# One-core attention and channel mix: shorter weight conversion, one 64-column transpose for the last keys, a split first gate, new load order

## The chip, the cores and the metric

The kernel runs on one core of a Trainium2 chip. The metric is the device time in microseconds of one execution; shown is the median of several. The core's engines are TensorE (PE; its weight loads are the rows PEld), VectorE (DVE), ScalarE (ACT), GpSimd (POOL) and SyncE (SP), which here issues nearly all DMAs. Each engine runs its own instructions in order and waits for others by semaphores. Sums of matmuls land in PSUM.

## The reference, cut to what matters

```python
B, H, S, D = 8, 8, 576, 64;  pool = 8
k_p = k.reshape(B, H, 72, 8, D).mean(axis=3)          # 72 pooled keys per head
v_p = v.reshape(B, H, 72, 8, D).mean(axis=3)
attn = softmax(q @ k_p.T / sqrt(D))                   # 576 x 72 per head
x = (attn @ v_p), heads side by side                  # 8 x 576 x 512
x_prev = x shifted by one position along the sequence (zeros first)
xk = mu_k * x + (1 - mu_k) * x_prev
xr = mu_r * x + (1 - mu_r) * x_prev
h = relu(xk @ w_k) ** 2                               # 512 -> 1024
out = sigmoid(xr @ w_r) * (h @ w_v)                   # 1024 -> 512
```

All is float32 to the caller. w_k, w_v and w_r come to the device as 64-bit floats.

## The kernel before, in words

The 4608 positions are cut into 12 chunks of 384, each of three tiles of 128 positions (tiles 0 to 35). For a tile, `softmax` multiplies q by the pooled keys of its batch into the PSUM pair `sc`, and DVE, ACT and POOL form the probabilities: `pm` for the first 64 keys of each head, `px` for the last 8. `transposed` turns `pm` round on TensorE (four transposes, L667) and writes it as a high and a low part. `transposed_rest` does the same for `px`: DVE first writes `pr`, three copies side by side (high, low, high; two casts at L698 and a subtraction at L700), TensorE transposes it as two blocks of 96 columns (L706), and one ACT cast (L713) writes `ptr`.

For a chunk, `attended` multiplies by the pooled values (L749, four groups of columns g), `shifted` makes xk and xr on ACT, POOL and DVE (L762 to L781), and `x_parts` splits them into high and low parts. Then come `hidden` (L825, eight blocks jt, each over four groups ct), `gate` (L874, three tiles over four blocks of w_r) and `mixed` (L906, three tiles over eight blocks of w_v). Every product is made of three matmuls of split operands (high by high, high by low, low by high), each one pass through TensorE; the split parts have the type float32r. Chunk 0 is the exception: `WHOLE = (0,)` makes its products one float32 matmul each, which TensorE runs as two slower passes, so that it need not wait for split weights.

The weights are 20 blocks of 512 KB (8 of w_k, 4 of w_r, 8 of w_v). `convert` makes float32 of a block: one ACT activation (L427) and four DVE steps (L429, L431, L436, L441). `split` later makes the high part (ACT, L463) and the low part (DVE or POOL as `LOW_BY` says, L466). The pooled sums of keys and values are made on TensorE, DVE or POOL, as `SUM_BY` says (L484 on TensorE, L473 on the others).

The order of instructions on each engine is fixed when the program is built: a planner (`Order`) plays generators, one for each step, against assumed durations and due times, and emits what would start first. `LOADS` is the order of the first 37 loads on SP's queue; in it k0 is the first half of batch 0's keys, v and r stand for values, q for a tile's queries, wk3 for the fourth block of w_k. Three PSUM banks called `bank` are shared by transposes and `attended`, three called `mm` by the products, and `sc` takes two.

Of the kernel before, what the change touches and what calls it, by code (L numbers as in the profile page):

```python
# [10 lines left out]
I32 = mybir.dt.int32  # L11
AF = mybir.ActivationFunctionType
# [4 lines left out]
P = 128  # L17
# [6 lines left out]
DM = H * D  # L24
# [5 lines left out]
WBUFS = 2 * NJT + NCT + 1  # L30
# [4 lines left out]
WHOLE = (0,)  # L35

TINY = 2.0**-15
# [6 lines left out]
SUM_BY = {  # L44
    "k0": "t", "k1": "v", "v0": "t", "v1": "t", "r0": "t", "k2": "v", "k3": "v", "v2": "g", "v3": "g",
    "r1": "g",
}

NORM_BY = {0: "v", 1: "v", 2: "v", 3: "v"}
WARMING = 4  # L50
FILL = (([("scored", 1)], 8),)

LOW_BY = {"k": "gvgvgvgv", "r": "gvgv", "v": "gvgggvgv"}
BY_HEAD = (0, 2)
# [3 lines left out]
COPIES_ON_ACT = 0  # L58

EARLIER = {  # L60
# [3 lines left out]
}  # L64
# [5 lines left out]

class Order:

    LATENCY = {"pe": 0.195, "dve": 0.13, "act": 0.14, "pool": 0.1, "sp": 0.0}

    def __init__(self):  # L80
        self.free = dict.fromkeys(self.LATENCY, 0.7)
        self.port = dict.fromkeys(self.LATENCY, 0.0)
        self.landed = 0.0
        self.now = 0.0
        self.made = {}
        self.slots = {}
        self.threads = []
        self.table = "exp"

    def add(self, due, steps, spare=0.0):  # L90

        given = [str(v) for v in steps.gi_frame.f_locals.values() if isinstance(v, (int, str))]
        due += EARLIER.get(" ".join([steps.gi_code.co_name, *given]), 0.0)
        self.threads.append([due, 0.0, None, steps, ("", 0.0), spare])

    def make(self, what, at=None):
        self.made[what] = self.now if at is None else at

    def give(self, kind, slot):
        self.slots.setdefault(kind, []).append((self.now, slot))  # L100

# [5 lines left out]
    @staticmethod  # L107
    def wait(t, until):
        t[1], t[4] = max(t[1], until), (t[4][0], max(t[4][1], until))

    def settle(self, t):

        while t[2] is None or t[2][0] in ("need", "take"):
            if t[2] is None:
                reply = None
            elif t[2][0] == "need":
                if any(w not in self.made for w in t[2][1:]):
                    return True
                self.wait(t, max(self.made[w] for w in t[2][1:]))
                reply = None  # L120
            else:
                have = self.slots.get(t[2][1])
                if not have:
                    return True
                at, reply = min(have, key=lambda h: h[0])
                have.remove((at, reply))
                self.wait(t, at)
            self.now = t[1]
            try:
                t[2] = t[3].send(reply)  # L130
            except StopIteration:
                return False
        return True

    def run(self):
        while True:
            self.threads = [t for t in sorted(self.threads, key=lambda t: t[0]) if self.settle(t)]
            ready = []
            for t in self.threads:
                if t[2][0] in ("need", "take"):  # L140
                    continue
                eng, _, lock = t[2][:3]
                at = max(
                    self.free[eng],
                    t[4][1] if t[4][0] == eng else t[1] + (t[5] if eng == "pe" else 0.0),
                )
                if lock:
                    at = max(at, self.port["pool" if eng == "dve" else "dve"])
                ready.append((at, t))
            if not ready:  # L150
                assert not self.threads, [t[2] for t in self.threads]
                return
            first = min(at for at, _ in ready)
            eng = next(t for at, t in ready if at == first)[2][0]
            at, t = min(
                ((at, t) for at, t in ready if t[2][0] == eng and at <= first + 0.1),
                key=lambda c: c[1][0],
            )
            _, length, lock = t[2][:3]
            func = t[2][3] if len(t[2]) > 3 else None  # L160
            if func and func != self.table:
                length, self.table = length + 1.3, func
            self.free[eng] = at + length
            if lock:
                self.port[eng] = at + length

            t[4] = (eng if eng == "pe" else "", at + length)
            t[1] = self.now = at + length + self.LATENCY[eng]
            try:
                t[2] = t[3].send(None)  # L170
            except StopIteration:
                self.threads.remove(t)


def dve(n, lock=True):
    return "dve", 0.05 + n / 960, lock
# [10 lines left out]
def pe(n, whole=False, times=1):  # L187
    return "pe", times * (2 * max(0.111, n / 1200 + 0.003) if whole else max(0.111, n / 2400 + 0.0155)), False
# [3 lines left out]
def attention_then_channel_mix(  # L192
# [41 lines left out]
    vbd_w = sb.tile([P, NPAIR, P], F32, name="vbd_w", tag="xkl")  # L234
# [16 lines left out]
    slots("rs", CH // P, [P, DM])  # L251
# [78 lines left out]
    def warm():  # L330
# [5 lines left out]
        for _ in range(WARMING):  # L336
            yield "pe", 0.86, False
# [39 lines left out]
    def load(kind, i):  # L377
# [37 lines left out]
    def convert(kind, i):  # L415
# [7 lines left out]
        low_word, top = w[:, :, 0], w[:, :, 1]  # L423
        ff = yield take("tmp")
        t = ff.bitcast(I32)
        yield act(WP)
        nc.scalar.activation(out=ff, in_=top.bitcast(F32), func=AF.Abs)  # L427
        yield "dve", 0.335, True
# [6 lines left out]
        yield dve(WP)  # L435
        nc.vector.scalar_tensor_tensor(  # L436
            out=t, in0=top, scalar=-0x40000000, in1=t, op0=ALU.bitwise_and, op1=ALU.bitwise_or
        )
# [571 lines left out]
```

## Time and profile before

| | us |
|---|---|
| median of 3 runs | 636.03 (635.59 to 637.77) |
| the profiled execution's own time | 637.05 |
| its span, first to last instruction | 635.3 |
| PE busy | 621.9 |
| DVE busy | 413.9 |
| ACT busy | 334.4 |
| POOL busy | 215.8 |

The profile's view of 40 slices shows the DMA engines at nine tenths or more only in the first three slices (to about 48 us) and PE at nine tenths from the third slice nearly to the end. The view of waits lists who ended an engine's idle time; the timeline lists instructions in order of time; the view by windows gives the busy time of each engine in a stretch. Matmuls overlap in their ends, so the distance from start to start, and not the duration, says what one costs in a stream.

### The profile page before, as it was taken

The page shows a single profiled execution, that of the slowest core. Times are in us where ns is not written, and L with a number is a line of the kernel's source. Part 1 is how long each engine was busy: PE and PEld are TensorE (multiplying, and loading weights), DVE is VectorE, ACT ScalarE, POOL GpSimd, SP SyncE. Part 2 cuts the span into 40 slices and gives each one's busy share as a digit, 9 for nine tenths or more (in the row PEclk, how much of TensorE's full clock was granted, in tenths as well). Part 3 has the DMA queues.
Part 4 walks back from the last instruction along what each step waited for, and adds up shares of the span by engine and source line. Part 5 has one row for each costly group of instructions (what it writes and reads, how often), then busy time and mean ns, then how long its engine had stood idle before and what let it go on. Part 6 is the DMA issues. An engine that isn't in the chain of part 4 may idle for free.

```text
span 635.3 us, 9068 instructions
## 1 busy us (share of the span) xinstructions
PE 621.9 (98%) x3256; PEld 538.6 (85%) x3256; DVE 413.9 (65%) x830; ACT 334.4 (53%) x688; POOL 215.8 (34%) x331
## 2 busy tenths in 40 slices
PE   7899999999999999999999999999999999999997
PEld 6754468889989989989988988988988988988986
DVE  5999998856979537647845665855854654653421
ACT  4667656855665644645454555546555455444420
POOL 1240348464435128028115018316405105203100
PEclk9999999999999999999999999999999999999999
DMA  9991130043314111033011061033110100000001
GB/s 293 364 390 62 33 125 35 15 126 142 91 51 172 61 35 51 0 142 108 17 35 51 0 202 49 16 109 125 33 34 34 35 17 34 18 0 35 18 0 50
DMA packets 35132, 50.91 MB, mean 80 GB/s; under 512 B 6544, under 2 KB 23184, under 8 KB 35088
## 3 DMA queue, kind: packets, MB, share of 16 engines
q1 hardware_dynamic: 34944, 50.22, 23.5%
q8 instruction: 25, 0.41, 0.3%
q14 instruction: 19, 0.16, 0.1%
q10 hardware_dynamic: 144, 0.13, 0.1%
HBM read 40.90 MB, written 9.44 MB: 79 GB/s over the span
## 4 chain that ended last, share of the span: by engine, by line
PE 84%; DMA 6%; DVE 5%; POOL 2%; SPq 1%; issue 1%; ACT 0%; DVEq 0%; POOLq 0%; ACTq 0%
PE mm L906 28%; PE mm L825 28%; PE mm L874 15%; PE bank L749 5%; PE sc L592 4%; DMA qs<-in_qT 4%; PE bank L667 2%; DMA got_wv<-in_w_v 1%; DMA got_wr<-in_w_r 1%; PE bank L706 1%; DVE tmp L436 1%; SPq L397 1%; POOL xkl L799 0%; DVE tmp L429 0%; POOL w_r L466 0%
## 5 line engine op out<-in xcount | busy, mean ns | idle before, releaser
L825 PE MATMUL mm<-xkh,w_k 128*128 128x384 f32 x704 | 182.2, 339 | 0.3 <-ACT xkh L797 0.3
L906 PE MATMUL mm<-w_v,sh 128*128 128x512 f32 x528 | 170.8, 392 | 0.0
L825 PEld LDWEIGHTS mm<-xkh,w_k 128*128 128x128 f32 x704 | 125.6, 188 | 1.5 <-issue 0.6
L825 PE MATMUL mm<-xkl,w_k 128*128 128x384 f32 x352 | 118.1, 336 | 0.7 <-POOL xkl L799 0.7
L906 PEld LDWEIGHTS mm<-w_v,sh 128*128 128x128 f32 x528 | 99.2, 188 | 19.8 <-issue 0.2
L906 PE MATMUL mm<-w_v,sl 128*128 128x512 f32 x264 | 103.0, 390 | 0.0
L642 POOL TENSOR_TENSOR px<-e,sm 128x64 f32<-128x64 f32 x32 | 11.4, 356 | 225.3 <-DVE sm L636 225.2
L874 PE MATMUL mm<-w_r,xrh 128*128 128x512 f32 x264 | 84.9, 394 | 0.0
L762 ACT ACTIVATE t<-bank,om_sb 128x384 f32<-128x384 f32 x96 | 48.8, 582 | 56.2 <-PE bank L749 56.1
L848 ACT CAST sh<-rk 128x384 fp32r<-128x384 f32 x88 | 45.2, 514 | 58.2 <-DVE rk L842 58.1
L781 DVE SCALAR_TENSOR_TENSOR xm<-bank,mu_sb,t 128x384 f32<-128x384 f32 x88 | 51.4, 612 | 35.2 <-POOL t L774 18.3
L850 DVE TENSOR_TENSOR sl<-rk,sh 128x384 fp32r<-128x384 f32 x88 | 53.5, 611 | 25.6 <-ACT sh L848 25.6
L825 PEld LDWEIGHTS mm<-xkl,w_k 128*128 128x128 f32 x352 | 66.1, 188 | 1.3 <-POOL xkl L799 1.3
L920 DVE TENSOR_TENSOR rs<-mm,rs 128x512 f32<-128x512 f32 (+1 forms) x37 | 24.8, 673 | 61.4 <-PE mm L906 61.4
L842 DVE SCALAR_TENSOR_TENSOR rk<-mm,rk 128x384 f32<-128x384 f32 x88 | 48.5, 553 | 16.4 <-ACT rk L835 15.8
L874 PEld LDWEIGHTS mm<-w_r,xrh 128*128 128x128 f32 x264 | 49.6, 188 | 10.0
L799 POOL TENSOR_TENSOR xkl<-xm,xkh 128x384 fp32r<-128x384 f32 x44 | 44.8, 1021 | 37.0 <-ACT xkh L797 36.6
L906 PEld LDWEIGHTS mm<-w_v,sl 128*128 128x128 f32 x264 | 49.7, 188 | 9.0
L473 POOL TENSOR_TENSOR stage<-stage 128x512 f32<-128x512 f32 (+5 forms) x60 | 51.0, 857 | 14.1 <-DMA stage<-in_vm 6.6
L835 ACT ACTIVATE rk<-mm 128x384 f32<-128x384 f32 x88 | 42.9, 488 | 23.3 <-PE mm L825 22.7
L874 PE MATMUL mm<-w_r,xrl 128*128 128x512 f32 x132 | 51.4, 389 | 0.0
L605 DVE TENSOR_REDUCE mx<-sc 128x8 f32<-128x576 f32 x35 | 26.3, 752 | 31.4 <-PE sc L592 31.4
(117 smaller groups left out, 979.2 us busy)
## 6 DMA issues: line engine op xcount, KB each, us to landing
out<-rs SPq DMA_DIRECT2D x35, 256.0 KB, 2.0
stage<-in_kT SPq DMA_DIRECT2D x15, 576.0 KB, 5.0
qs<-in_qT SPq DMA_DIRECT2D x32, 256.0 KB, 3.2
stage<-in_vm SPq DMA_DIRECT2D x14, 512.0 KB, 6.5
got_wk<-in_w_k SPq DMA_DIRECT2D x8, 512.0 KB, 9.2
got_wv<-in_w_v SPq DMA_DIRECT2D x8, 512.0 KB, 10.0
stage<-in_vr SPq DMA_DIRECT2D x7, 384.0 KB, 4.1
got_wr<-in_w_r SPq DMA_DIRECT2D x4, 512.0 KB, 8.3
```

The lines of the kernel that those rows point to most:

```text
L473: nc_eng.tensor_tensor(out=st[:, :, :w], in0=st[:, :, :w], in1=st[:, :, w:2 * w], op=ALU.add)
L749: nc.tensor.matmul(out=xp[:, o], lhsT=v, rhs=p, start=(q == 0), stop=(q == len(terms) - 1))
L762: nc.scalar.activation(out=t[:, m, 1:n + 1], in_=xp, func=AF.Copy, scale=om_sb[:, m, g:g + 1])
L781: nc.vector.scalar_tensor_tensor(out=xm[:, :n], in0=xp, scalar=mu_sb[:, m, g:g + 1], in1=t[:, m, :n], op0=ALU.mult, op1=ALU.add,)
L799: nc.gpsimd.tensor_tensor(out=lo, in0=xm[:, :n], in1=hi, op=ALU.subtract)
L825: nc.tensor.matmul(out=hp, lhsT=w[:, o], rhs=x[:, ct, :n], start=(ct == 0 and k == 0), stop=(ct == NCT - 1 and k == len(terms) - 1),)
L835: nc.scalar.activation(out=rk[:, :n], in_=hp, func=AF.Relu)
L842: nc.vector.scalar_tensor_tensor(out=rk[:, :n], in0=hp, scalar=0.0, in1=rk[:, :n], op0=ALU.max, op1=ALU.mult)
L848: nc.scalar.copy(out=sh[:, :n], in_=rk[:, :n])
L850: nc.vector.tensor_tensor(out=operand("sl", c)[:, jt, :n], in0=rk[:, :n], in1=sh[:, :n], op=ALU.subtract)
L874: nc.tensor.matmul(out=bank, lhsT=x[:, ct, o], rhs=w, start=(ct == 0 and k == 0), stop=(ct == NCT - 1 and k == len(terms) - 1),)
L906: nc.tensor.matmul(out=bank, lhsT=s[:, o], rhs=w, start=(jt == 0 and k == 0), stop=(jt == NJT - 1 and k == len(terms) - 1),)
```

## The change

The change has these parts:

- `convert`: the clamp (L429) and one of the two-tensor steps go. ACT scales by 2^-112 while it takes the absolute value; DVE moves three bits of the low word by one 16-bit shift in place (TENSOR_SCALAR, every fourth 16-bit word), shifts the result by 3 (TENSOR_SCALAR), and joins it with the top word (one SCALAR_TENSOR_TENSOR).
- `transposed_rest`: `px` is transposed once, as 64 columns, into one bank; the high, low and high rows are then made from the bank by two ACT casts, two DVE subtractions and two more ACT casts, each of 32 partitions by 128.
- `WHOLE` is now a set of stages: the gate of chunk 0 takes split operands, so the four blocks of w_r and the xr of chunk 0 are split early, and `attended` of chunk 0 needs the buffer `xrl` free.
- `LOADS`, `SUM_BY`, `NORM_BY`, `LOW_BY`, `BY_HEAD` and the dummy matmuls (`FILLS`: 6 in place of 8) are new, the planner is rewritten, and weight buffers are now numbered slots.

```diff
-WHOLE = (0,)
+WHOLE = {"p", "k", "v"}
 LOADS = (
-    "k0 k1 q0 q1 wk0 v0 v1 wk1 c0 q2 r0 wk2 wk3 k3 wk4 v3 v2 q3 wk5 r1 k2 wk6 wk7 q4 wr0 q5 wr1 wr2 "
-    "wr3 wv0 wv1 wv2 wv3 wv4 wv5 wv6 wv7 "
+    "k0 k1 wk1 q0 q1 wk5 q2 v0 v1 k3 v2 c0 r0 q5 wk0 k2 wk2 wr3 q3 wv6 wv7 v3 wr1 q4 wk4 wk3 "
+    "wk7 r1 wr2 wk6 wv3 wv1 wv2 wr0 wv4 wv0 wv5 "
 )
...
-FILL = (([("scored", 1)], 8),)
+FILLS = ((("scored", 1), 6),)
...
     def convert(kind, i):
...
-        nc.scalar.activation(out=ff, in_=top.bitcast(F32), func=AF.Abs)
-        nc.vector.tensor_scalar(out=ff, in0=ff, scalar1=TINY, scalar2=None, op0=ALU.max)
+        nc.scalar.activation(out=ff, in_=top.bitcast(F32), func=AF.Abs, scale=DOWN)
         nc.vector.tensor_scalar(
-            out=t, in0=t, scalar1=3, scalar2=0x3FFFFFF8,
-            op0=ALU.logical_shift_left, op1=ALU.bitwise_and,
+            out=quarters[:, :, 2], in0=quarters[:, :, 1], scalar1=13, scalar2=None,
+            op0=ALU.logical_shift_right,
         )
-        nc.vector.scalar_tensor_tensor(
-            out=t, in0=top, scalar=-0x40000000, in1=t, op0=ALU.bitwise_and, op1=ALU.bitwise_or
-        )
+        nc.vector.tensor_scalar(out=t, in0=t, scalar1=3, scalar2=None, op0=ALU.logical_shift_left)
         nc.vector.scalar_tensor_tensor(
-            out=got[:, :WP], in0=low_word, scalar=29, in1=t,
-            op0=ALU.logical_shift_right, op1=ALU.bitwise_or,
+            out=got[:, :WP], in0=top, scalar=-0x7FFFFFF9, in1=t, op0=ALU.bitwise_and, op1=ALU.bitwise_or
         )
...
-    def transposed_rest(i):
+    def transposed_rest(c, first, n):
...
-        for k in (0, 2):
...
-                nc.vector.tensor_copy(out=pr[:, :, k], in_=px)
-        nc.vector.tensor_tensor(out=pr[:, :, 1], in0=px, in1=pr[:, :, 0], op=ALU.subtract)
-        for r in range(2):
-            nc.tensor.transpose(
-                out=rp[:REM, r, :],
-                in_=pr[:, r].bitcast(F32).rearrange("p c h k -> p (c h k)"),
-                identity=ident,
-            )
-        nc.scalar.copy(out=operand("ptr", c)[:, :, o], in_=rp[:REM, :2, :])
+            nc.tensor.transpose(
+                out=bank[:8 * KR, j * P:(j + 1) * P], in_=px.rearrange("p a h k -> p (a h k)"), identity=ident
+            )
+        for r in range(2):
+            nc.scalar.copy(out=ptr[:rows, r, o], in_=rp[r * rows:(r + 1) * rows])
+        for r in range(2):
+            nc.vector.tensor_tensor(
+                out=ptr[rows:2 * rows, r, o], in0=rp[r * rows:(r + 1) * rows], in1=ptr[:rows, r, o],
+                op=ALU.subtract,
+            )
+        for r in range(2):
+            nc.scalar.copy(out=ptr[2 * rows:, r, o], in_=rp[r * rows:(r + 1) * rows])
```

The first place is SP's queue around the load of wk3. In the kernel before, wk3 is the fourteenth load:

```order
L397 DMA got_wk2_161<-in_w_k 128x1024
L397 DMA got_wk3_166<-in_w_k 128x1024
L411 DMA early_ptl_110<-in_kT 128x1152
L397 DMA got_wk4_174<-in_w_k 128x1024
L411 DMA early_xrl_111<-in_vm 128x1024
```

In the changed kernel it is the twenty-seventh row, behind wk4, and batch 1's first keys (`stage0`) come before wk2:

```order
L424 DMA got_wk0_180<-in_w_k 128x1024
L438 DMA stage0_105<-in_kT 128x1152
L424 DMA got_wk2_191<-in_w_k 128x1024
L424 DMA got_wr3_195<-in_w_r 128x1024
L414 DMA qs1_103<-in_qT 128x4x128
L424 DMA got_wv6_207<-in_w_v 128x1024
L424 DMA got_wv7_221<-in_w_v 128x1024
L438 DMA stage1_106<-in_vm 128x1024
L424 DMA got_wr1_228<-in_w_r 128x1024
L414 DMA qs2_104<-in_qT 128x4x64 x2
L424 DMA got_wk4_249<-in_w_k 128x1024
L424 DMA got_wk3_260<-in_w_k 128x1024
```

Blocks of w_r and w_v have moved ahead of most of w_k.

The second place is PE at the start of `attended` for chunk 0 (`bank` from `pth`, the transposed probabilities). The kernel before:

```order
L484 MATMUL mm1_117<-early_sl_109,ident_64 96x128 x8
L667 MATMUL bank0_113<-ident_64,pm0_90 128x128 x4
L706 MATMUL bank1_114<-ident_64,pr0_94 96x128 x2
L749 MATMUL bank2_115<-pth_0_240,vbd_w_75 128x384
L749 MATMUL bank2_115<-ptr_0_249,vbd_r0_76 128x384
L749 MATMUL bank0_113<-pth_0_240,vbd_w_75 128x384
L749 MATMUL bank0_113<-ptr_0_249,vbd_r0_76 128x384
L592 MATMUL sc0_112<-kbd0_69,qs0_103 128x144 x4
L825 MATMUL mm2_118<-xkh_0_362,got_wk0_136 128x384
```

The changed kernel:

```order
L713 MATMUL bank2_114<-ident_64,px2_93 64x128
L686 MATMUL bank0_112<-ident_64,pm0_89 128x128 x4
L500 MATMUL mm0_115<-stage0_105,ident_64 128x144 x8
L769 MATMUL bank1_113<-pth_0_246,rs0_77 128x384
L769 MATMUL bank1_113<-ptr_0_227,vbd_r0_75 128x384
L769 MATMUL bank0_112<-pth_0_246,rs0_77 128x384
L769 MATMUL bank0_112<-ptr_0_227,vbd_r0_75 128x384
L609 MATMUL sc0_111<-kbd0_69,qs1_103 128x144 x4
L845 MATMUL mm2_117<-xkh_0_371,got_wk0_180 128x384
```

The sums of k2 (eight matmuls from `stage0`) now stand between the last transposes and `attended`, and one transpose of `px` stands where two of `pr` stood.

The third place is PE from the last blocks of `hidden` in chunk 0 to its gate. The kernel before:

```order
L825 MATMUL mm1_117<-xkh_0_362,got_wk2_161 128x384
L825 MATMUL mm2_118<-xkh_0_362,got_wk3_166 128x384 x4
L825 MATMUL mm0_116<-xkh_0_362,got_wk4_174 128x384 x4
L825 MATMUL mm1_117<-xkh_0_362,got_wk5_202 128x384 x4
L825 MATMUL mm2_118<-xkh_0_362,got_wk6_268 128x384 x4
L825 MATMUL mm0_116<-xkh_0_362,got_wk7_278 128x384 x4
L874 MATMUL mm1_117<-got_wr0_299,xrh_0_366 128x512
L874 MATMUL mm1_117<-got_wr1_312,xrh_0_366 128x512
```

The changed kernel, right behind the eight score matmuls of tile 4:

```order
L609 MATMUL sc0_111<-kbd1_70,qs2_104 64x144
L845 MATMUL mm2_117<-xkh_0_371,got_wk3_260 128x384 x4
L845 MATMUL mm1_116<-xkh_0_371,got_wk4_249 128x384 x4
L845 MATMUL mm0_115<-xkh_0_371,got_wk5_138 128x384 x4
L845 MATMUL mm2_117<-xkh_0_371,got_wk6_297 128x384 x4
L845 MATMUL mm1_116<-xkh_0_371,got_wk7_265 128x384 x4
L713 MATMUL bank0_112<-ident_64,px3_94 64x128
L686 MATMUL bank2_114<-ident_64,pm1_90 128x128 x4
L713 MATMUL bank1_113<-ident_64,px0_91 64x128
L609 MATMUL sc0_111<-kbd1_70,qs0_102 128x144 x4
L896 MATMUL mm0_115<-w_r0_527,xrh_0_380 128x512
L896 MATMUL mm0_115<-w_r0_527,xrl_0_381 128x512
```

The scores of tiles 4 and 5 and the transposes of tile 3 have moved ahead of the gate, and the gate reads the split `w_r0` in place of `got_wr0`.

## Rows read from the trace of the kernel before

**Rows 1.** Windows: us, busy by engine (instructions), granted clock, DMA share, GB/s.
```profile
30.00:40.00 10.00, 8.98 (x29) 5.20 (x28) 9.68 (x20) 6.17 (x16) 6.34 (x12) 1.00 1.06 372
...
200.00:300.00 100.00, 100.00 (x543) 91.06 (x542) 59.92 (x119) 51.67 (x106) 37.61 (x57) 1.00 0.20 66
```

**Rows 2.** Waits of PE: line, releaser: us in total, times, longest.
```profile
PE mm L825 <- DVE xkh L781: 2.0, 2, 1.0
...
PE mm L874 <- DVE got_wr L441: 1.3, 1, 1.3
...
PE mm L825 <- POOL xkl L799: 0.7, 2, 0.5
...
PE bank L706 <- DVE pr L700: 0.4, 1, 0.4
PE mm L825 <- ACT xkh L797: 0.3, 1, 0.3
PE mm L906 <- DVE got_wv L441: 0.2, 1, 0.2
```

**Rows 3.** Timeline of PE, chunk 0: start us, us, what [idle before].
```profile
25.31 0.91 PE L749 MATMUL bank<-pth,vbd_w 128*128 128x384 f32 x2 [0.58 <-ACT pth L675]
...
29.26 1.56 PE L825 MATMUL mm<-xkh,got_wk 128*128 128x384 f32 x4 [0.98 <-DVE xkh L781]
...
37.99 15.10 PE L825 MATMUL mm<-xkh,got_wk 128*128 128x384 f32 x46 [1.02 <-DVE xkh L781]
...
56.95 7.99 PE L874 MATMUL mm<-got_wr,xrh 128*128 128x512 f32 x18 [1.28 <-DVE got_wr L441]
64.78 0.60 PE L667 MATMUL bank<-ident,pm 128*128 128x128 f32 x4
65.21 0.38 PE L706 MATMUL bank<-ident,pr 128*96 128x128 f32 x2
65.43 1.88 PE L906 MATMUL mm<-got_wv,sh 128*128 128x512 f32 x4
```

**Rows 4.** The chain that ended last, the last chunk's gate: start us, us.
```profile
606.88 8.20 PE mm L874 x36
```

**Rows 5.** Groups of DVE by shape: busy us, mean ns | idle before.
```profile
L431 DVE TENSOR_SCALAR tmp<-tmp 128x512 int32<-128x512 int32 x20 | 9.3, 472 | 0.0
...
L436 DVE SCALAR_TENSOR_TENSOR tmp<-got_wv,tmp 128x512 int32<-128x512 int32 x8 | 5.5, 688 | 0.0
```

**Rows 6.** SP issues with time to landing: v3, then wr0, then wr1.
```profile
L411 SPq DMA_DIRECT2D early_xrl<-in_vm x1: 431/431/431, 14.0 to 14.0; - x1
...
DMA to landing us min/median/max: 10.4/10.4/10.4
...
L397 SPq DMA_DIRECT2D got_wr<-in_w_r x1: 3747/3747/3747, 27.0 to 27.0; - x1
...
DMA to landing us min/median/max: 9.8/9.8/9.8
...
L397 SPq DMA_DIRECT2D got_wr<-in_w_r x1: 617/617/617, 31.4 to 31.4; - x1
...
DMA to landing us min/median/max: 7.5/7.5/7.5
```

**Rows 7.** Groups by shape on ACT and DVE, columns as in Rows 5.
```profile
L427 ACT ACTIVATE tmp<-got_wk 128x512 f32<-128x512 f32 x8 | 5.4, 679 | 2.4 <-DMA got_wk<-in_w_k 1.4 <-DVE got_wk L441 1.0
...
L713 ACT CAST ptr<-bank 96x256 fp32r<-96x256 f32 x36 | 13.3, 370 | 0.2 <-PE bank L706 0.2
...
L553 ACT CAST vq<-mm 96x128 fp32r<-96x128 f32 x1 | 0.3, 262 | 0.0
...
L555 DVE TENSOR_TENSOR vq<-mm,vq 32x128 fp32r<-32x128 f32 x1 | 0.3, 289 | 0.1
```

**Rows 8.** Windows of one us, columns as in Rows 1.
```profile
14.00:15.00 1.00, 0.00 (x0) 0.00 (x0) 0.65 (x3) 0.90 (x2) 0.00 (x0) 1.00 1.04 238
...
16.00:17.00 1.00, 1.00 (x6) 1.00 (x6) 0.54 (x4) 0.00 (x0) 0.00 (x0) 0.50 1.02 381
```

More of the change, by code (lines that the diff above doesn't have):

```diff
@@ L105, in fetched, with advance @@
         self.make(what, self.landed)
[L107 to L128, printed above, removed]
+    def advance(self, t):
+        while True:
+            reply = None
+            if t.step is not None:
+                if t.step[0] == "need":
+                    for w in t.step[1:]:
+                        if w not in self.made:
+                            self.waiting.setdefault(w, []).append(t)
+                            return
+                    until = max([self.made[w] for w in t.step[1:]])
+                else:
+                    have = self.slots.get(t.step[1])
+                    if not have:
+                        self.takers.setdefault(t.step[1], []).append(t)
+                        return
+                    until, reply = got = min(have, key=lambda h: h[0])
+                    have.remove(got)
+                t.at = max(t.at, until)
+                if t.pe_at is not None:
+                    t.pe_at = max(t.pe_at, until)
+            self.now = t.at
@@ L129, in settle @@
             try:
-                t[2] = t[3].send(reply)
+                t.step = t.steps.send(reply)
             except StopIteration:
-                return False
-        return True
-    def run(self):
[L136 to L145, printed above, removed]
-                )
[L147 to L157, printed above, removed]
-            )
[L159 to L162, printed above, removed]
@@ new lines, in advance, with stretch @@
+                return
+            if t.step[0] not in ("need", "take"):
+                self.ready.append(t)
+                return
+    def stretch(self, at, length):
+        if at > 60:
+            return length
+        self.bursts = [b for b in self.bursts if b[1] > at - self.WINDOW]
+        busy = sum(b[1] - max(b[0], at - self.WINDOW) for b in self.bursts) / self.WINDOW
+        if busy < 0.39:
+            self.slow = True
+        elif busy > 0.93:
+            self.slow = False
+        length *= 1 + self.slow
+        self.bursts.append((at, at + length))
+        return length
@@ L261, in attention_then_channel_mix @@
     slots("vq", 1, [REM, 2, D], F32R)
+    for i in range(WSLOTS):
+        order.give("w", i)
     slots("tmp", 2, [P, WP])
@@ L468, in split @@
         )
+        order.give("w", held.pop(("slot", kind, i)))
         order.make(("parts", kind, i))
@@ L533, in values @@
         order.make(("values", b, p))
[L534 to L535 removed]
+        if as_is:
+            yield need(("attended", 0))
             yield act(2 * P)
@@ L541, in values @@
             )
-            order.make(("value parts", b, p))
-        else:
-            order.make(("value parts", b, p))
+            held["spent", p] = True
+            if ("spent", 1 - p) in held:
+                order.give("rs", for_rs[0])
+        order.make(("value parts", b, p))
     def last_values(b):
@@ L714, in transposed_rest @@
         order.give("bank", bank)
-        order.make(("side", i))
+        for j in range(n):
+            order.make(("side", first + j))
     def attended(c, g):
         n = CHUNKS[c]
-        whole = c in WHOLE
+        as_is = whole(c, "p")
         mine = [i for i, t in enumerate(tiles) if t[0] == c]
```

236 lines of the change are left out of this document (136 added, 100 removed), and 3 rows, old and new, of the table EARLIER.

## The prediction

> **What bounds the kernel now.** I read the windows first, then PE's waits, PE's timeline and the chain. From 150 us on PE is busy all the time (100.00 of 100.00 us in the window shown) while DVE has 60 of 100 and ACT 52 [rows 1]: there only less TensorE work makes the kernel shorter. Before that PE loses time in two ways. Up to 37.99 us chunk 0 waits for its data: `hidden` starts at 29.26 and waits for the fourth x block until 37.99 [rows 3], with DVE busy 9.68 of 10 us and the DMA engines at 1.06 [rows 1]. From 37.99 on PE works nearly without a gap; its waits there sum to 1.3 + 0.7 + 0.4 + 0.3 + 0.2 = 2.9 us, and two waits for DVE's x blocks, 2.0 us, lie ahead of it [rows 2].
>
> **The transposes.** Two transposes start at 65.21 and the next matmul at 65.43, four start at 64.78 and end their turn at 65.21 [rows 3]: 0.11 us each, whatever they turn. Of 72 in the whole run 36 go. Those of tiles 0 to 2 lie in the stretch where PE waits anyway and count nothing; 33 x 0.11 = 3.6 us less.
>
> **The gate of chunk 0.** Its last 18 instructions take 64.78 - 56.95 = 7.83 us, 0.435 each [rows 3]; the 24 of the gate make 10.45 us. Split, it is 36 instructions, as in the last chunk, where they take 8.20 us [rows 4]. 2.25 us less.
>
> **The conversion.** A block costs DVE two TENSOR_SCALAR (0.47) and two SCALAR_TENSOR_TENSOR (0.69) [rows 5]; now it costs two of the first kind, one of them 16-bit and strided, and one of the second. No row shows the 16-bit form. If it runs like the row of its kind the block saves 0.69 us, over 20 blocks 13.8 us of DVE; if it runs at the rate of the strided two-tensor row, 0.69, the saving is 9.4 us; at half of 0.47 it is 18.5. I take 0.47, the row of the same operation. The Trainium skill (VectorE: DVE Perf Modes, What auto-detection actually checks) says that a single-source operation between SBUF tensors gets two elements a cycle without being packed, and that the faster 16-bit form wants step one. By that rule the saving would be the 13.8 us too, by the strided row the 9.4.
> DVE is no bound after 38 us, except through the waits for converted weights, 1.3 + 0.2 us. Those go: the DVE work between 57 and 95 us shrinks by about 8 blocks x 0.69 = 5.5 us, and the two casts and the subtraction of `pr` give way to two subtractions of 32 x 128 out of PSUM, 0.289 in the one row there is [rows 7]. The wait of 0.4 for `pr` has no object any more. The waits for `xkl` and `xkh` in chunk 1 (0.7 + 0.3) go because `attended` of chunk 1 now ends ten slow matmuls of `mixed` earlier in PE's order, instead of right ahead of `hidden`. 2.9 us less, and I give back 0.5 for new short waits: `mixed` now reads wv5 and wv6 soon after DVE's step of joining them, which stands behind x blocks of chunk 1.
>
> **The split of w_r and xr, early.** It adds four casts and four subtractions, on ACT, POOL and DVE, ahead of the gate. wr0 is now load 35 of 37 with 15360 KB ahead of its end; after wr0's and wr1's rows below the stream moves 768 KB in 2.1 us, so it lands near 38.9 + 2.1 x 3584/768 = 48.7 [rows 6]. DVE then has its shifts and join among other steps, some 24 instructions of 0.2 to 0.7 us from 41.9 on (below), so the float32 block is there near 52.5. The gate begins at 41.9 + 20 x 0.656 (the last five blocks of `hidden`) + 1.6 (scores and transposes now ahead of it) = 56.6: some 4 us for a cast and a subtraction. Were this cover gone, the gate would wait, and all of `mixed` behind it.
>
> **The loads.** What lands is set by the bytes ahead. In the old order wr0 (11008 KB up to its end) was issued at 27.0 and landed 9.8 later, at 36.8; wr1 (11776 KB) at 31.4 + 7.5 = 38.9; v3 (6976 KB) at 14.0 + 10.4 = 24.4 [rows 6]. In the new order wk3 ends at 11392 KB, so it lands near 37.9 (it was at 5376 KB before), and k2 at 6784 KB, near 23.8. Two things hang on that.
> First, `attended` of chunk 0 stands behind the sums of k2 in PE's order: 16 passes of about 0.12 (the transposes above take 0.11), so 25.8 instead of 25.31 [rows 3]. On the other side DVE does less between the first and the fourth x block: in its old order a TENSOR_SCALAR and a join of conversions stand between them (0.47 + 0.69), in the new one only sums of keys. I take the fourth x block 1.0 us earlier, at 37.0; between 1.5 later (k2 late, ACT's queue held by the wk2 activation) and 2.5 earlier (q2 comes some 3 us sooner).
> Second, `hidden` needs wk3 right after three matmuls of 0.656 (46 passes in 15.10 us, two a matmul [rows 3]) and the scores of tile 4, 1.1: at 40.1. wk3 needs ACT's 0.68 [rows 7] and then, since DVE's order pairs it with wk4, three TENSOR_SCALAR and two joins, 2.8, with an x block of 0.5 between: 37.9 + 0.7 + 0.5 + 2.8 = 41.9. A new wait of 1.7 us, from 0 (landing a little sooner) to 4.
>
> **The sum.** The profiled execution took 637.05, its span 635.3 of it. -3.6 - 2.25 - 2.9 + 0.5 - 1.0 + 1.7 = -7.55 gives 629.5. That execution was 1.0 above the median of 636.03, so the median should come to 628.5. The scores of tiles 4 and 5 only change places. Two dummy matmuls fewer lie in the waiting stretch and cost nothing.
>
> **Rivals.**
> The start gains more: the fourth x block 2.5 earlier and wk3 in time. -3.6 - 2.25 - 2.9 - 2.5 = -11.25: 624.8. For it speaks q2, up from the eleventh load to the seventh; against it that k2's sums stand ahead of `attended` now. Chance 0.10.
> The loads come late: 1.5 later at the fourth x block, a wait of 4 for wk3. -3.6 - 2.25 - 2.9 + 0.5 + 1.5 + 4.0 = -2.75: 633.3. For it: the DMA engines are full until 48 us; against it: the bytes fix the landing within about a microsecond. Chance 0.14.
> The clock: at 14 to 15 us PE did nothing, and the granted clock fell from 1.00 to 0.50 (2.4 to 1.2 GHz) soon after, for a stretch around 16 to 18 us [rows 8]. The new order leaves PE idle at other places before `attended`; one such stretch of three microseconds inside `hidden` would cost 1.7, two would cost 3.4: 630.2 to 632. The Trainium skill (TensorE: Matmul & The Clock Gate, Why this matters for your kernels) warns against idle gaps between bursts of matmuls; the row agrees. Chance 0.06.
> Slower: the way of `px` out of its bank is now six steps on two engines in place of one cast of 0.37. Nearest rows: 4 x 0.262 + 2 x 0.289 = 1.63 [rows 7], 1.26 more a tile. `attended` waits for the last tile's `ptr`, and three banks serve all. If ACT and DVE are too far behind to do it under PE's work, each of 11 chunks would pay the 1.26 at the last tile and some queue: 11 x 1.26 = 13.9, so 642.4. Half of that leaves 0.6 us of the gain. It decides where fewer than about 2 us of PE work lie between the last transpose and the fourth matmul of `attended`. Against it: PE's order has at least 24 matmuls of 0.228 there, 5.5 us, ACT is half idle, and PE has no idle time in the late window of the old order [rows 1]. Chance 0.08.
>
> **The numbers.** Forecast 0.62, early gain 0.10, late loads 0.14, clock 0.06, slower 0.08. The median time is 628.5; the range 624.5 to 633.5 holds all but the last case and the ends. A difference below 0.3%, 1.9 us, can't be told from none: faster 0.87 (all but the slower case and a third of the late loads), within 0.05, slower 0.08.
>
> **What would show it.** In the profile after: 36 transposes of 64 columns; the gate of chunk 0 in 36 instructions of 8.2 us without a wait ahead; a wait of PE for wk3's joining step near 40 us; no PE wait after 105 us; the 16-bit TENSOR_SCALAR near 0.47. Wrong would be: PE waits for `ptr` casts behind 120 us, `attended` of chunk 0 after 27 us, or the gate waiting for `w_r0`.

## The result and the profile after

The changed kernel takes 640.73 us (median of 7; 638.52 to 641.08) against 637.13 for the kernel before beside it: a ratio of 1.005, 95% interval 1.0032 to 1.0069. It is slower by half a per cent, where 628.5 was forecast. The profiled execution took 638.52, the shortest of the seven, with a span of 636.7.

What answers to [rows 1], columns the same: late in the run PE is as full as before and DVE too. The stretch that changed is 40 to 55 us. In the kernel before PE was busy 15.00 of 15 us there and POOL 2.59:

```profile
40.00:55.00 15.00, 15.00 (x46) 8.55 (x45) 14.83 (x34) 11.10 (x23) 2.59 (x1) 1.00 0.70 273
```

In the changed kernel PE has 10.02 of 15 us there, DVE 13.92 and POOL 5.14; from 60 to 82 us DVE is busy 20.47 of 22.

```profile
200.00:300.00 100.00, 100.00 (x547) 90.61 (x546) 59.78 (x119) 57.22 (x127) 36.49 (x56) 1.00 0.25 83
40.00:55.00 15.00, 10.02 (x40) 5.85 (x39) 13.92 (x26) 8.61 (x19) 5.14 (x6) 0.89 0.76 283
60.00:82.00 22.00, 19.21 (x86) 13.22 (x84) 20.47 (x38) 17.71 (x43) 8.55 (x7) 1.00 0.32 113
```

The waits of PE, which answer to [rows 2]. Those for `got_wr`, `pr`, `xkl` and `xkh` of chunk 1 are gone as forecast. In their place stand longer ones; the first, put down to "issue", ends 0.1 us after DVE's join of wk3 (below).

```profile
PE mm L845 <- issue: 5.0, 1, 5.0
PE mm L845 <- DVE xkh L801: 2.7, 2, 1.7
PE mm L928 <- DVE got_wv L465: 2.2, 2, 1.6
PE bank L713 <- DVE px L661: 2.0, 2, 1.1
```

PE's timeline, which answers to [rows 3]: `attended` at 25.65, a wait for the third x block until 36.28, the wait for wk3, the gate from 63.08 to 71.38 without a wait ahead (8.30 us; [rows 4] had 8.20), then three short waits, and chunk 1's `hidden` at 103.35. In the kernel before that began at 95.20.

```profile
25.65 0.81 PE L769 MATMUL bank<-pth,rs 128*128 128x384 f32 x2
...
36.28 4.78 PE L845 MATMUL mm<-xkh,got_wk 128*128 128x384 f32 x14 [0.98 <-DVE xkh L801]
...
47.18 14.52 PE L845 MATMUL mm<-xkh,got_wk 128*128 128x384 f32 x40 [4.98 <-issue]
...
63.08 0.48 PE L896 MATMUL mm<-w_r,xrh 128*128 128x512 f32 x1
...
71.38 0.60 PE L686 MATMUL bank<-ident,pm 128*128 128x128 f32 x4
73.12 0.30 PE L713 MATMUL bank<-ident,px 128*64 128x128 f32 x1 [1.14 <-DVE px L661]
...
78.59 2.84 PE L928 MATMUL mm<-got_wv,sh 128*128 128x512 f32 x6 [1.61 <-DVE got_wv L465]
...
93.23 8.85 PE L928 MATMUL mm<-got_wv,sh 128*128 128x512 f32 x20 [0.63 <-DVE got_wv L465]
...
103.35 0.61 PE L845 MATMUL mm<-xkh,w_k 128*128 128x384 f32 x2
```

The block awaited until 36.28 is the third, not the fourth as in [rows 3]: DVE writes it from 35.61 to 36.23 and the fourth from 38.00 to 38.61, while PE is at the 14 passes. Between the second and the third block DVE sat idle for 2.38 us. It waited for POOL, which first made a low part of xr (33.19 to 34.19) and a sum (34.15). Later ACT's step for wk3 begins only at 40.45, behind a cast of xr that waited for DVE. wk3 itself had landed near 36.0 (issued at 28.05, 7.9 us to landing). DVE, POOL and ACT:

```profile
35.61 0.62 DVE L801 SCALAR_TENSOR_TENSOR xkh<-bank,mu_sb,t 128x384 f32<-128x384 f32 x1 [2.38 <-POOL t L793]
...
38.00 0.61 DVE L801 SCALAR_TENSOR_TENSOR xkh<-bank,mu_sb,t 128x384 f32<-128x384 f32 x1
```

```profile
34.15 1.27 POOL L489 TENSOR_TENSOR stage<-stage 128x512 f32<-128x512 f32 x1
```

```profile
40.04 0.51 ACT L817 CAST xrh<-xm 128x384 fp32r<-128x384 f32 x1 [1.19 <-DVE xm L801]
40.45 0.66 ACT L455 ACTIVATE tmp<-got_wk 128x512 f32<-128x512 f32 x1
```

DVE and then POOL in the wait for wk3 (timeline of each). Two shift steps take 2.33 us and two joins 2.79, just while POOL sums the last values of batch 1 (L489) and forms `pm` (L667).

```profile
41.15 1.09 DVE L457 TENSOR_SCALAR got_wk<-got_wk 128x512 uint16<-128x512 uint16 x1 [0.83 <-ACT tmp L455]
42.03 2.33 DVE L462 TENSOR_SCALAR tmp<-tmp 128x512 int32<-128x512 int32 x2
44.28 2.79 DVE L465 SCALAR_TENSOR_TENSOR got_wk<-got_wk,tmp 128x512 int32<-128x512 int32 x2
```

```profile
41.59 3.09 POOL L489 TENSOR_TENSOR stage<-stage 96x512 f32<-96x512 f32 x3
...
44.89 1.03 POOL L667 TENSOR_TENSOR pm<-e,sm 128x512 f32<-128x512 f32 x1
```

The conversion's groups on DVE, which answer to [rows 5]: the 16-bit step L457 has a mean of 783 ns for w_k and 1003 for w_v, not 470.

```profile
L462 DVE TENSOR_SCALAR tmp<-tmp 128x512 int32<-128x512 int32 x20 | 11.3, 575 | 0.0
L457 DVE TENSOR_SCALAR got_wv<-got_wv 128x512 uint16<-128x512 uint16 x8 | 7.6, 1003 | 0.4 <-ACT tmp L455 0.4
L465 DVE SCALAR_TENSOR_TENSOR got_wk<-got_wk,tmp 128x512 int32<-128x512 int32 x8 | 6.9, 877 | 0.0
L465 DVE SCALAR_TENSOR_TENSOR got_wv<-got_wv,tmp 128x512 int32<-128x512 int32 x8 | 6.6, 835 | 0.0
L457 DVE TENSOR_SCALAR got_wk<-got_wk 128x512 uint16<-128x512 uint16 x8 | 6.3, 783 | 2.3 <-ACT tmp L455 2.3
```

As in [rows 8], the clock falls behind an idle PE: windows of one us around the end of the wait.

```profile
46.00:47.00 1.00, 0.00 (x0) 0.00 (x0) 1.00 (x3) 0.00 (x0) 0.00 (x0) 0.78 1.01 401
47.00:48.00 1.00, 0.82 (x2) 0.55 (x3) 0.97 (x3) 0.89 (x2) 0.00 (x0) 0.50 1.03 410
```

### The profile page after: what moved, and what is told of

The parts are those of the page before. It is cut to its first block, busy times and chain, and to the rows that moved or that the text cites. A ratio compares the mean times of both kernels' runs of the same rounds, so it can differ in the third digit from the quotient of the medians.

```text
span 636.7 us, 9067 instructions
## 1 busy us (share of the span) xinstructions
PE 614.9 (97%) x3228; PEld 535.5 (84%) x3228; DVE 397.7 (62%) x769; ACT 358.1 (56%) x798; POOL 220.4 (35%) x339
## 4 chain that ended last, share of the span: by engine, by line
PE 87%; DVE 5%; ACT 4%; issue 1%; DMA 1%; POOL 1%; SPq 0%; DVEq 0%; POOLq 0%
PE mm L845 31%; PE mm L928 30%; PE mm L896 14%; PE bank L769 5%; PE sc L609 5%; PE bank L686 2%; DMA got_wk<-in_w_k 1%; ACT e L633 1%; ACT tmp L455 1%; DVE got_wv L457 1%; DVE got_wv L465 1%; PE bank L713 1%; POOL xrl L819 0%; ACT t L781 0%; DVE xm L801 0%
## 5 line engine op out<-in xcount | busy, mean ns | idle before, releaser
L896 PE MATMUL mm<-w_r,xrh 128*128 128x512 f32 x288 | 92.9, 396 | 0.0
L801 DVE SCALAR_TENSOR_TENSOR xm<-bank,mu_sb,t 128x384 f32<-128x384 f32 x92 | 53.1, 612 | 53.2 <-POOL t L793 34.3
L896 PEld LDWEIGHTS mm<-w_r,xrh 128*128 128x128 f32 x288 | 54.1, 188 | 11.7
L489 POOL TENSOR_TENSOR stage<-stage 128x512 f32<-128x512 f32 (+6 forms) x66 | 56.0, 864 | 11.0 <-DMA stage<-in_vm 9.8
L896 PE MATMUL mm<-w_r,xrl 128*128 128x512 f32 x144 | 56.1, 390 | 0.0
L819 POOL TENSOR_TENSOR xrl<-xm,xrh 128x384 fp32r<-128x384 f32 x48 | 48.6, 1013 | 7.2 <-ACT xrh L817 7.0
```

The source lines that it names most:

```text
L489: nc_eng.tensor_tensor(out=st[:, :, :w], in0=st[:, :, :w], in1=st[:, :, w:2 * w], op=ALU.add)
L801: nc.vector.scalar_tensor_tensor(out=xm[:, :n], in0=xp, scalar=mu_sb[:, m, g:g + 1], in1=t[:, m, :n], op0=ALU.mult, op1=ALU.add,)
L819: nc.gpsimd.tensor_tensor(out=lo, in0=xm[:, :n], in1=hi, op=ALU.subtract)
L896: nc.tensor.matmul(out=bank, lhsT=x[:, ct, o], rhs=w, start=(ct == 0 and k == 0), stop=(ct == NCT - 1 and k == len(terms) - 1),)
```

## The experiments

Theory P: DVE's steps stretch while POOL works, so every operand it makes between 40 and 82 us is late. Rivals: theory L, wk3 lands too late; theory C, the fallen clock is what costs; theory D, DVE's chain is simply too long for the new order. Times are medians of runs beside the kernel before, with the ratio's 95% interval. The kernel before had medians of 636.4 to 637.1 us in these sets, so a difference between kernels of two sets is good to about 0.7 us.

**A quiet POOL at 42 us.** The changed kernel with POOL's sums of r1 and the `pm` of tile 3 cut to four columns.

```diff
+        if light:
+            nc_eng.tensor_tensor(out=st[:, :, :4], in0=st[:, :, :4], in1=st[:, :, w:w + 4], op=ALU.add)
+            return
```

> The changed kernel with the same order of instructions, but GpSimd's three sums of batch 1's last values and its product for tile 3's first 64 keys work on 4 columns only (their results are left out; both stand beside the conversion of wk3). Theory P (GpSimd and VectorE get in each other's way in SBUF): VectorE's two shifts and two joins for wk4 and wk3, 2.33 and 2.79 us in the changed kernel, fall to about 0.75 and 1.3; wk3 is ready near 43.8 instead of 47.1, PE's wait of 4.98 us shrinks to 1.5 to 2, the clock does not fall behind it, and the time is 4 to 6 us below the changed kernel's 640.7, so 635 to 637. Theory L (wk3 is loaded too late): the wait and the time stay as they are.

The rest of these sums and weights is left out. Measured 636.97 us, ratio 1.0002 (0.9988 to 1.0017): 3.8 below the changed kernel (3.1 by the ratios). DVE's same four steps:

```profile
43.03 0.78 DVE L462 TENSOR_SCALAR tmp<-tmp 128x512 int32<-128x512 int32 x2
43.73 1.38 DVE L465 SCALAR_TENSOR_TENSOR got_wk<-got_wk,tmp 128x512 int32<-128x512 int32 x2
```

They take 2.16 us in place of 5.12. PE's wait for wk3 falls from 4.98 to 2.04, and the 40 passes behind it run at full clock, but a later wait has grown from 1.14 to 3.27:

```profile
45.22 13.14 PE L849 MATMUL mm<-xkh,got_wk 128*128 128x384 f32 x40 [2.04 <-ACT sh L865]
...
72.81 0.42 PE L717 MATMUL bank<-ident,px 128*64 128x128 f32 x1 [3.27 <-DVE px L664]
```

So P holds for the stretch of wk3's chain, and part of the gain was given back. (The 2.04 too ends 0.1 us after DVE's join, at 45.11; ACT's step is only the last the view knows of.)

**wk3 loaded earlier.** The loads of wk3 and wv6 change places.

```diff
+            kind, i = {("wk", 3): ("wv", 6), ("wv", 6): ("wk", 3)}.get((kind, i), (kind, i))
```

> The changed kernel with the DMAs of wk3 and wv6 changing places on SP's queue (wk3 six loads earlier), all else the same. Theory L (the load order makes wk3 late): PE's wait before the wk3 block falls from 5.0 us by 2 or more, and the time by as much. Theory P: wk3 has long landed when ScalarE comes to it at 40.45 us, so the wait stays within 0.5 us of 5.0 and the time within 1 us of the changed kernel's 640.7.

Measured 639.65 us, 1.0043 (1.0026 to 1.0061). PE's wait is 4.98 us again and DVE's four steps take 2.33 and 2.79 as before. Theory L falls.

```profile
47.18 15.75 PE L847 MATMUL mm<-xkh,got_wk 128*128 128x384 f32 x40 [4.98 <-issue]
```

**A busy wait.** 22 dummy matmuls of float32 ahead of the fourth hidden block.

```diff
+        if c == 0 and jt == 3:
+            for _ in range(22):
+                nc.tensor.matmul(out=bank[:, :P], lhsT=ident, rhs=ident, start=True, stop=True)
```

> The changed kernel with 22 dummy float32 matmuls (128 columns, about 0.22 us each) in TensorE's order right ahead of the wk3 block, where it waits 5 us. Theory C (part of the loss is the granted clock falling to half behind that wait): PE is busy through the wait, the clock stays at 1.00 from 46 to 51 us, the 40 instructions behind it take 13.1 instead of 14.5 us, and the time falls by 1.4 us or a little more (in other runs the mean clock was lower than in the profiled one), to 638 to 639.5. Without theory C: time the same or up to 0.5 us longer.

Measured 641.45 us, 1.0071 (1.0056 to 1.0087). PE's timeline:

```profile
43.18 5.18 PE L836 MATMUL mm<-ident 128*128 128x128 f32 x44
48.19 13.16 PE L848 MATMUL mm<-xkh,got_wk 128*128 128x384 f32 x40
...
75.82 0.30 PE L713 MATMUL bank<-ident,px 128*64 128x128 f32 x1 [3.29 <-DVE px L661]
```

The clock stays at 1.00 and the 40 passes take 13.16 instead of 14.52, so the fallen clock costs 1.4 us there; but PE then waits 3.29 us for `px`, 2.15 more than before. Keeping PE busy gains nothing while DVE is behind. Theory C falls as the cause.

**The old order.** The kernel before with the new conversion and the new transposes, its order kept.

> The kernel before, its old order of loads and of instructions and its whole-precision first gate kept, with two parts of the change alone: the conversion in three VectorE steps, and the single 64-column transpose with six evictions. My sum: 33 transposes of 0.11 less = 3.6 us, and the waits on conversions (1.3 + 0.2 us) mostly gone: 4 to 5 us below before, 632 to 633.5. If the transposes and evictions bring nothing or cost (the chain out of the bank): 636 or more.

Measured 636.82 us, 1.0003 (0.9993 to 1.0012): no gain at all, and the expectation was wrong. PE in chunk 0, and what ACT does ahead of it:

```profile
25.94 1.09 PE L667 MATMUL bank<-ident,pm 128*128 128x128 f32 x4 [2.69 <-ACT vbd_w L524]
```

```profile
23.14 0.52 ACT L705 CAST ptr<-bank 32x128 fp32r<-32x128 f32 x2
24.30 0.52 ACT L712 CAST ptr<-bank 32x128 fp32r<-32x128 f32 x2 [0.64 <-DVE ptr L707]
24.83 1.07 ACT L524 COPY vbd_w<-mm 64x128 f32<-64x128 f32 x4
```

In order, ACT now waits for DVE's subtractions between its casts of `ptr`, the copy of the values stands behind them, and PE behind that. Behind this wait the granted clock is 0.50 until past 31 us, which costs PE more time. This is the forecast's slower rival, at work in chunk 0 only.

**All of POOL quiet.** As the first run, and also the sums of batch 2's first keys and the low parts of weights that POOL makes.

> The changed kernel with nearly all of GpSimd's early bulk work taken out: beside the sums of the last values of batch 1 and the weights of tile 3 (as in the experiment with a quiet GpSimd) also the sums of the keys of batch 2, and the low parts of weights that GpSimd made (4 columns of each are left, and TensorE reads the high part in their place), so its output is not the reference's; matmuls, VectorE and ScalarE steps stay the same. Theory P (VectorE's steps stretch while GpSimd works, and every late operand of 40 to 82 us comes of that): in the experiment before, the wait merely moved to the transpose at 72.8 us (3.3 us and a slow clock behind it, some 2 us more), because four VectorE steps between 58 and 70 us took 1.1 to 1.3 us longer beside GpSimd. With that gone I expect 632 us (630.5 to 634), no VectorE step of a 128x512 form over 0.9 us between 38 and 82 us, and the wait for px under 0.5 us. Theory D (the chain of steps itself is too long for the new order): 636 to 637.5, the px wait stays above 2 us.

TensorE reads the high part in place of the low parts left out. Measured 633.26 us, 0.9945 (0.9923 to 0.9967): as theory P has it. The wait for `px` is 0.30 us, and DVE's 60 conversion steps sum to 39.0 us where the changed kernel has 44.4.

The run does not separate two effects: POOL disturbs DVE less, and PE and DVE no longer wait for what POOL itself makes. It is still 4.8 us above the forecast, and the wait for wk3 is 2.03 as in the first run.

**Three pieces put later.** The sums of r1 and tile 3's `pm` wait in the plan for the conversion of wk3, batch 2's sums for tile 4.

```diff
+        if b == 1:
+            yield need(("full", "k", 3))
```

> The changed kernel with three pieces of work put later and nothing left out: the sums of the last values of batch 1 and the weights of tile 3 wait for the conversion of the fourth hidden weight, the sums of the keys of batch 2 for the weights of tile 4. The planner lays the rest out anew, so other places shift as well. Theory P: the wait of 5.0 us before the fourth hidden block falls to about 2, the step chain before the transpose at 72 us is no longer stretched by the sums of keys (1.2 us), so 636 to 638 us against 640.7 of the changed kernel. Theory D: as the changed kernel, 640 to 641.

Measured 646.8 us, 1.0143 (1.0112 to 1.0174). It tells nothing on POOL at 42 us: the edit changed the plan, but nothing stood between on POOL's queue, so the sums ran where they had been (the row below) and the wait stayed at 4.98 us. The rest of the plan became worse (PE waits 3.6 us for w_v's blocks).

```profile
41.84 3.09 POOL L489 TENSOR_TENSOR stage<-stage 96x512 f32<-96x512 f32 x3
```

**The transposes alone, from chunk 1 on.** The kernel before; chunk 0 keeps the old form of `transposed_rest`.

```diff
+        if c:
+            bank = yield take("bank")
+            nc.tensor.transpose(out=bank[:8 * KR, :P], in_=px.rearrange("p a h k -> p (a h k)"), identity=ident)
...
+            return
```

> The kernel before with one part of the change alone, from the second chunk on: the last keys transposed as 64 columns and split behind it; chunk 0, the conversion and the order stay as before. By the prediction's own term (33 transposes by 0.11 us) 3.3 to 3.6 us less than before: 633.3 us. If the longer chain of evictions (seven short steps on two engines instead of one cast) delays `attended` in the chunks behind, the gain is lost: 636 to 637.

Measured 635.78 us, 0.999 (0.9975 to 1.0004). From chunk 1's `hidden` (96.89) to the end the profile has 633.0 - 96.9 = 536.1 us, where the kernel before has 635.3 - 95.2 = 540.1: the 3.6 are there. Ahead of it 1.7 us are lost; PE's waits for `got_wv`, 0.2 in [rows 2], sum to 2.3.

**The same with the new conversion.**

> As the run with the transposes from the second chunk on, and the new conversion of weights in three VectorE steps as well, still in the order of before. The conversion takes 0.27 us of VectorE's time per weight (one of four steps) away. If that is worth what the prediction takes the gate's wait for (1.3 us), the result is 632; if the strided 16-bit step gives it back (0.73 us in place of 0.42, seen in the changed kernel) and two waits for v's weights come (1.7 us in all in the experiment with the old order), it is 633 to 634.5, no better than the transposes alone.

Measured 632.35 us, 0.9931 (0.9908 to 0.9954). Here the conversion is worth 3.4 us: the gate's wait of 1.29 is gone, and DVE's conversion steps sum to 37.9 us against 44.9 in the kernel before. Against the old-order run the difference is chunk 0's form of `transposed_rest`: 4.5 us. (The old-order run, these two and the last one have four `px` buffers in place of two, as the changed kernel has.)

**The whole gate.** The changed kernel with chunk 0's gate from float32 operands.

```diff
-WHOLE = {"p", "k", "v"}
+WHOLE = {"p", "k", "v", "r"}
```

> The changed kernel with chunk 0's gate from whole float32 operands again, as before; the planner lays the work behind it out anew. If the prediction's term for this edit is right by itself (36 split matmuls in 8.2 us against 24 whole ones in 10.46 us), this kernel is 2.25 us slower than the changed one: 643. If the casts and low parts that the split operands need ahead of the gate (4 each for w_r, 4 low parts of x on GpSimd) stretch VectorE's steps and so give the gain back in the waits of 72 to 80 us, it is 638 to 641, no slower.

Measured 645.21 us, 1.0131 (1.0106 to 1.0156): slower than the changed kernel by 4.5. The whole gate takes 10.55 us, the split one 8.30, so the gate by itself gains the forecast's 2.25. What the split is worth in all, the run does not settle, since the order differs. Without it the whole gate begins 3.4 us sooner (59.70, 63.08 in the changed kernel). Of that 1.4 us are a tile's transposes and scores, which the changed kernel does ahead of its gate. The third x block comes 4.5 us behind the first (6.1 in the changed kernel) and PE does not wait for it. The whole gate ends at 70.09, 1.3 us before the split one. The loss comes behind it, with waits of 1.03 and 1.45 us for w_v's blocks and 1.66 for scores.

**r1 loaded last**, so that POOL cannot sum it at 42 us.

```diff
-    "wk7 r1 wr2 wk6 wv3 wv1 wv2 wr0 wv4 wv0 wv5 "
+    "wk7 wr2 wk6 wv3 wv1 wv2 wr0 wv4 wv0 wv5 r1 "
```

> The changed kernel with nothing left out and one load put last in the early list: the last values of batch 1, so that GpSimd cannot sum them while VectorE finishes the fourth hidden weight; the weights and loads behind it land a little earlier. Theory P: the two shift steps before the join take 0.8 us and not 2.3, the wait of 5.0 us falls to 3 or less, and the time is 637 to 639.5. Theory D (not GpSimd): wait and time stay, 640 to 641.

Measured 641.63 us, 1.0076 (1.0055 to 1.0096). The wait for wk3 fell to 2.79, as P has it, and the time did not:

```profile
45.44 13.14 PE L845 MATMUL mm<-xkh,got_wk 128*128 128x384 f32 x40 [2.79 <-ACT sh L861]
...
62.94 0.66 PE L686 MATMUL bank<-ident,pm 128*128 128x128 f32 x4 [2.73 <-DVE ptl L699]
```

The sums of r1 went to 57 to 65 us, where DVE's steps stretch (a `pm` 1.76 us in place of 0.69), and the gate now waits 1.57 us for w_r. Moving the collision does not take it away.

**A contiguous 16-bit step.** The changed kernel; the shift works on a scratch tile, the rest is the same instruction for instruction. The weights lose their lowest three bits, and the shift needs neither the block nor ACT's step any more.

```diff
-            out=quarters[:, :, 2], in0=quarters[:, :, 1], scalar1=13, scalar2=None,
+            out=scratch[:, WP:], in0=scratch[:, :WP], scalar1=13, scalar2=None,
```

> The changed kernel with the 16-bit step of the conversion on a contiguous scratch tile (512 elements in, 512 out) in place of every fourth half-word of the weights; the weights lose their lowest three bits, all else is the same instruction for instruction. If the stride sets the step's 0.73 us, it falls to 0.4 us or less, as the contiguous 32-bit step has, and the chains at 45 and 72 us shorten by some 0.3 us for each step on them: 639 to 640. If 16-bit integers are slow by themselves, it stays at 0.73 us and the time at 640 to 641.

Measured 633.69 us, 0.994 (0.9918 to 0.9963): 7 us below the changed kernel, far more than either case expected. DVE's groups and PE's timeline:

```profile
L459 DVE TENSOR_SCALAR flat<-flat 128x512 uint16<-128x512 uint16 x20 | 7.1, 353 | 0.1
```

```profile
43.30 13.14 PE L847 MATMUL mm<-xkh,got_wk 128*128 128x384 f32 x40 [2.06 <-ACT sh L863]
...
67.37 0.30 PE L715 MATMUL bank<-ident,px 128*64 128x128 f32 x1 [0.69 <-DVE px L663]
...
71.58 2.84 PE L930 MATMUL mm<-got_wv,sh 128*128 128x512 f32 x6 [0.35 <-DVE got_wv L467]
...
96.30 0.60 PE L847 MATMUL mm<-xkh,w_k 128*128 128x384 f32 x2
```

The step falls from 16.8 us in all to 7.1, every wait behind it shrinks, the clock stays, and chunk 1 begins 7.05 us sooner. POOL's sums are still there. So the collision alone does not make the waits: DVE has little slack between 40 and 82 us, and what is added to it lands on PE. That is nearer to theory D than I had allowed. The stride is not the only thing that this edit takes away. For wk3 the shift now runs at 38.67, ahead of ACT's step at 38.89; in the changed kernel it waited 0.83 us for that step and ran behind it (41.15). How much of the 7 us is the stride and how much the freer order, no run shows.

**The best of both.** The order of before, the transposes from chunk 1 on, the conversion without its 16-bit step.

```diff
-        nc.vector.tensor_scalar(
-            out=quarters[:, :, 2], in0=quarters[:, :, 1], scalar1=13, scalar2=None,
-            op0=ALU.logical_shift_right,
-        )
...
-            out=got[:, :WP], in0=top, scalar=-0x7FFFFFF9, in1=t, op0=ALU.bitwise_and, op1=ALU.bitwise_or
+            out=got[:, :WP], in0=top, scalar=-0x80000000, in1=t, op0=ALU.bitwise_and, op1=ALU.bitwise_or
```

> The best of what the runs point to: the order of before, the 64-column transposes from the second chunk on, and the new conversion without its 16-bit step (two VectorE steps a block; the lowest three bits of every weight's fraction are zero, all else is as in the reference). In the run with the strided step VectorE's joins were late for v's weights (waits of 1.7 us in all) and the x blocks (1.5 us). If the strided step's 0.75 us is what made them late, those for v go and the time is 629.5 to 631; if they come of GpSimd's collisions or of ScalarE, it stays at 632 to 633.

Measured 631.65 us, 0.9923 (0.9903 to 0.9944), the lowest of all. Its median is 0.7 below the version that keeps the three bits, and the intervals of the two overlap, so that difference is not settled; both beat the kernel before and the changed one. The waits for `got_wv` went only from 1.7 to 1.3, so the strided step was not all that made v's weights late.

## Why the prediction was wrong, point by point

- Transposes, -3.6: right, where it could be seen apart (-4.0 from chunk 1 on, in the run of the transposes alone). That those of tiles 0 to 2 count nothing held in the new order (`attended` at 25.65, forecast 25.8), not in the old one, where the new way out of the bank cost chunk 0 4.5 us.
- Gate, -2.25: right for the gate itself, 36 instructions in 8.30 us with no wait. The work that it needs ahead was counted only at the gate, as cover of some 4 us; it told earlier, at the x blocks and on ACT's queue (below).
- **The step that failed is "DVE is no bound after 38 us, except through the waits for converted weights", and with it the price of the conversion**: "I take 0.47, the row of the same operation", 13.8 us less of DVE. PE's waits showed no bound, but DVE was busy 14.83 of 15 us from 40 to 55. The strided step took 0.73 to 0.75 us by itself, above the upper bound of 0.69, and 0.84 in the mean; beside POOL the other steps stretched too (L462 575 ns in the mean, 418 for the same shift in the last run). DVE's conversion steps sum to 44.4 us where the kernel before has 44.9: 0.5 saved, not 13.8. The same steps in the old order saved 7.0, and with POOL quiet in the new order 5.9. So about half of the 13.8 went to the step's own price, and the rest to what the new order puts beside it. No term stood for POOL's work beside DVE's, though the kernel before has such a step: L431 took 1.52 us at 63.76, where its mean is 0.47 [rows 5], while POOL worked from 63.73 to 65.00.
- The wait for wk3, +1.7: 4.98, 3.3 more than forecast. The sum had wk3 ready at 41.9, the trace has 47.07. Of these 5.2 us 3.1 are the chain of "three TENSOR_SCALAR and two joins, 2.8", which took from 41.15 to 47.07, 5.9. With POOL quiet it took 3.0, so that working was right for a DVE left alone. The other 2.1 are its start, 41.15 in place of 37.9 + 0.7 + 0.5 = 39.1: wk3 had landed, near 36.0, but ACT stood behind casts of xr. With POOL quiet this part stays, and the wait is still 2.04. The range of 0 to 4 knew only the landing, which was not at fault. That the split of xr is what held ACT is read from the rows; no run takes it out with the order kept.
- "2.9 us less, and I give back 0.5": the named waits did go, but new ones of 1.14 for `px` and 1.61 and 0.63 for `got_wv` came, 3.4 in all: 2.9 more than forecast.
- Clock: the rival's price was right in size. The long wait pulled it to 0.50, and the 40 passes behind took 14.52 us, not 13.14: 1.4. In the run with wk3 earlier, with the same wait, they took 15.75; such a longer fall would be 1.2 us of the 2.2 between the profiled execution and the median. The other 1.0 stays open; in the profile of the busy wait `hidden` begins 1.05 us later (31.21, not 30.16) with the same order up to there.
- The fourth x block, "1.0 us earlier, at 37.0", was ready at 38.61, where the kernel before has 37.93: 0.7 later. PE waited for the third instead, until 36.28, with only 10 of the 64 passes of `hidden` ahead of it, where [rows 3] have 4 + 4 + 10 = 18 ahead of 37.99. PE was 1.7 us sooner past its wait and had eight passes of 0.328 us more to do: +0.9 in place of -1.0. The forecast's "only sums of keys" looked at DVE's own steps and not at its wait for POOL, 2.38 us.
- The step from the profiled execution to the median, -1.0, was not there: it rested on three runs, and with seven the kernel before has a median of 637.13, as its profiled execution (637.05).

Together 3.3 + 2.9 + 1.4 + 1.9 = 9.5, against the 9.0 between 638.5 and the 629.5 of the sum. PE's view of waits names none behind 105 us, so the slower rival did not come about in the chunks behind: the evictions of `ptr` (72 casts each of 252 and 254 ns, 72 subtractions of 282) are hidden there, as argued.

## What to carry to other kernels

Before an engine is called "no bound", look at its busy share in the stretch where the consumer needs it: DVE was at 14.83 of 15 us from 40 to 55 us before the change, so it had nothing to spare, though PE never waited for it there. Price a step with its own access pattern and beside the work that will run next to it, not by the mean of a calm stretch; and where two engines disturb each other, count what the new order puts side by side. Try the parts of a change apart: here two of them (the transposes from chunk 1 on and the conversion) made 632.35 in the old order, and the rest of the change took it back. Which piece of that rest took how much is open.

## What the runs showed of the hardware that was not expected

A 16-bit shift of 512 elements, every fourth half-word in place, took 0.73 to 0.75 us; on contiguous half-words 0.24 to 0.29 where nothing disturbed it; the contiguous 32-bit shift 0.41. The Trainium skill (VectorE: DVE Perf Modes, What auto-detection actually checks) gives a single-source operation within SBUF two elements a cycle and asks for step one only for the faster 16-bit form: the contiguous case agrees, the strided one does not, being no faster than a two-source step (0.69). The measurement decides.

DVE's shifts and joins from SBUF to SBUF stop while POOL's TENSOR_TENSOR runs, rather than share. DVE and POOL of the changed kernel:

```profile
67.94 1.85 DVE L457 TENSOR_SCALAR got_wv<-got_wv 128x512 uint16<-128x512 uint16 x1
...
71.33 0.75 DVE L649 TENSOR_REDUCE sm<-e 128x8 f32<-128x576 f32 x1 [0.75 <-ACT e L647]
```

```profile
67.51 1.67 POOL L481 TENSOR_TENSOR w_r<-got_wr,w_r 128x512 fp32r<-128x512 f32 x1 [0.73 <-ACT w_r L478]
69.14 3.24 POOL L489 TENSOR_TENSOR stage<-stage 128x576 f32<-128x576 f32 x3
```

POOL's step ends at 69.18; DVE's, begun 0.43 behind it, ends 0.61 after that. Not every DVE step is held: the TENSOR_REDUCE at 71.33, with one operand in SBUF, ran inside POOL's three sums and took its usual 0.75 us. The Trainium skill (SBUF — State Buffer, Who interferes with whom) says that of a DVE step in a two-port mode and a GpSimd step the later is held until the first is over, and that a DVE step with one SBUF input outside these modes is not held. The int32 shifts and the reduce agree; the strided 16-bit step has one input and not the rate of a two-port mode (0.73 us, where the contiguous 32-bit shift has 0.41), and was held all the same. The measurement decides.
